# The first keys loaded in fp32 by SyncE's queue, a later running sum, and a reordered opening, in a fused forgetting-attention and MLP kernel

## The chip, the cores and the metric

The kernel runs on one core of one Trainium2 chip. The metric is the device time of one execution in microseconds (us). The time before is 321.48 us, the median of 3 runs (321.39 to 321.61). A profile is one further execution, recorded by the hardware; its span runs from the first to the last instruction.

## The reference

The first half is attention with a forget gate: B=8 batches, H=8 heads, S=576 positions, D=64. The second half is an MLP with a tanh-approximated GELU over the 4608 tokens, 512 to 2048 to 512. All inputs and outputs are fp32.

```python
scores = scale * np.matmul(q, k.transpose(0, 1, 3, 2))
log_f = np.log(np.clip(f, 0.0001, 1.0))
cum = np.cumsum(log_f, axis=-1)
decay = cum[:, :, :, None] - cum[:, :, None, :]
scores = np.where(causal, -1000000000.0, scores + decay)
attn = np.exp(scores - max) ; attn = attn / (np.sum(attn, axis=-1) + 1e-09)
x = (attn @ v) with the heads side by side          # 4608 x 512
h = x @ w_in
out = gelu_tanh(h) @ w_out
```

## The kernel before

**Attention.** Four heads are one quad; a batch has two quads, and 16 quads in all are numbered i. For a quad, q and k are loaded by GpSimd's queue (`load_one`, L205), which casts fp32 to bf16 on the way, into one of two buffers each (`k_c`, `q_c`). VectorE transposes them in blocks of 32 (`transpose_words`, L211) into `kT` and `qT`. TensorE multiplies 32 of the 64 columns of D at a time for four heads side by side in the rows of its array (`scores`, L265), into two PSUM tiles; ScalarE takes the exponential (L291) into `pt`, bf16. The causal mask on the diagonal blocks is set on GpSimd (`mask`, L293) or by a product on VectorE (`mask_by_product`, L317). The decay needs no work per score: the factor exp(-cum) of each key is multiplied into the values (`make_vw`, L227) and into the weights of the denominators (`w_bf`), and the factor of the query cancels in the division. For it, f is loaded by SyncE, clamped on VectorE, put through a logarithm on ScalarE (`logs`, L721), summed along each row on VectorE (`running_sums`, L725), transposed on TensorE (`cum_tiles`, L743) and exponentiated on ScalarE (`make_w`, L749). The denominators (`denominators`, L362) and the outputs (`attn_out`, L380) are products with `pt` in which the four heads lie side by side in the columns of the array; VectorE divides and writes x, transposed, into `xT`.

**MLP.** Tokens are worked on in nine chunks of 512. The first product runs by `mlp_in` (L388) or, for the first chunk, in halves of 256 tokens by `mlp_in_half` (L422); ScalarE takes the GELU into `gT`. The second product runs in units, for chunk 0 by `mlp_out` (L679) and from then on by `seven_products` (L603), which makes seven block products in place of eight and needs sums of the blocks of `gT` and `w_out` on VectorE. From chunk 2 on part of the first product uses the same scheme (`two_units`, L526).

**Order.** Each engine works through its own queue in order, and a program order written out by hand sets all of them. `setup` (L701) issues the first loads and constants; then `run` (L842) goes through tables of words: `FRONT` (L71) for everything up to chunk 2, `SECOND` for chunk 2, and so on. A word is an operation with its arguments. Those that matter here:

- `S.i.r` scores of round r of quad i; `H.i.r.g` the same for two of the four heads. Their matmuls use 32 rows of the array and 128 columns.
- `D`, `V`, `v` denominators and outputs (an argument 0 or 1 at the end is the first 256 or the last 320 positions); 128 rows and 32 columns, or one.
- `M` mask on GpSimd, `m` on VectorE. `VW` weighted values on GpSimd, `vw` on VectorE.
- `j`, `J`, `I` first product of the MLP; `GJ` its GELU where it is put off, `RJ` a copy of its raw sum. `F.c.n` n units of the second product of chunk c with 128 columns at a time, `f.c.n` the same units with four matmuls of 32 columns each.
- `B.n.c` n matmuls of c columns on zeros into a spare tile (`keep_busy`, L253); `BK` the same behind a transposed k (L259). They have no result.
- `SC` running sum, `CT` and `CE` its transposition and exponentials, `W`/`w` the cast of the factors. `TK`, `TQ` transpositions of k and q.
- Loads: `LK`, `LQ` of k and q; `LP` and `LC` of one piece of 128 positions of v for batch 0 and 1, by GpSimd's queue; `LV` of half of a v, by SyncE's; `WI`, `WO` pieces of w_in and w_out, by GpSimd's.
- `CL`, `cl` copy of one block of the weighted values, on VectorE or ScalarE; `UW`, `PW` a sum of blocks of w_in, on VectorE or GpSimd; `U` sums of w_out; `UT` and `tr` make the triangles for the mask.

The opening of `setup` and the issue of a load of k or q:

```python
nc.sync.dma_start(out=f_sb, in_=f.rearrange("b h s -> (b h) s"))          # L702
load_one(k, k_c, 0)                                                       # L704
load_one(q, q_c, 0)
```

PSUM has two tiles for scores (and the first product), one for products of a whole quad (the idle matmuls write it too) and two for the rest.

## Time and profile before

| | us |
|---|---|
| median of 3 runs | 321.48 |
| the profiled execution | 320.93 |
| its span | 319.2 |
| TensorE matmul busy | 313.2 (98%) |
| VectorE busy | 243.0 (76%) |
| ScalarE busy | 212.6 (67%) |
| GpSimd busy | 109.3 (34%) |

Matmuls are pipelined and their ends are modelled, so a busy TensorE is not one at its peak; starts are measured. The page cuts the span into 40 slices and shows in tenths how busy each engine was. The chain that ended last is followed back from the last instruction, each step to what released it. A row of a timeline gives start, duration, engine, line, operation, output<-input, the count of instructions merged into it, and in brackets how long the engine was idle before it and what ended that. PE is TensorE, PEld its weight loads, DVE VectorE, ACT ScalarE, POOL GpSimd, SP SyncE. A transfer has the time from its issue to its landing.

### The profile page before, as it was taken

What the parts mean: (1) busy time and instruction counts of PE and PEld (TensorE: products, weight loads), DVE (VectorE), ACT (ScalarE), POOL (GpSimd) and SP (SyncE); (2) the same over time, 40 slices, a digit from 0 to 9 for tenths busy, and PEclk for the clock granted to TensorE, in tenths of its full rate; (3) what the DMA queues carried; (4) which work ended last, traced back from release to release, by engine and by line L of the source; (5) the groups of instructions that cost most, each with busy time, mean ns of one, the idle gap of its engine ahead of it and who ended that gap; (6) DMA issues with size and microseconds to landing.
All of it is one profiled execution on the core that took longest, in us unless ns stands there. A gap on an engine that the chain in (4) does not pass through costs nothing.

```text
span 319.2 us, 11780 instructions
## 1 busy us (share of the span) xinstructions
PE 313.2 (98%) x5318; PEld 219.1 (69%) x5318; DVE 243.0 (76%) x369; ACT 212.6 (67%) x246; POOL 109.3 (34%) x148
## 2 busy tenths in 40 slices
PE   7999999999999999999999999999999999999996
PEld 2467734545676577776788878767776786688785
DVE  7777438598878889879877987599876866597674
ACT  3766885966766876877767866787596744836610
POOL 8799541920340416410851075305610140000000
PEclk9999999999999999999999999999999999999999
DMA  7999999985253901593139411961001111010203
GB/s 126 222 203 204 208 227 218 176 156 103 45 105 103 215 7 39 120 206 74 39 87 224 89 39 36 213 152 38 5 34 67 35 36 35 28 40 2 101 33 100
DMA packets 47490, 33.41 MB, mean 105 GB/s; under 512 B 29776, under 2 KB 42192, under 8 KB 47440
## 3 DMA queue, kind: packets, MB, share of 16 engines
q0 software_dynamic: 9632, 15.99, 28.8%
q1 hardware_dynamic: 37664, 16.60, 19.5%
q8 instruction: 41, 0.67, 0.9%
q10 hardware_dynamic: 144, 0.07, 0.1%
q14 instruction: 9, 0.07, 0.1%
HBM read 36.85 MB, written 9.44 MB: 145 GB/s over the span
## 4 chain that ended last, share of the span: by engine, by line
PE 94%; DMA 3%; POOL 1%; DVE 1%; issue 0%; DVEq 0%; POOLq 0%
PE ps_w L617 31%; PE ps_h L401 20%; PE ps_q L537 10%; PE po L353 9%; PE ps_s L283 9%; PE pso L690 5%; PE ps_h L437 5%; PE ps_u L485 4%; DMA v_nat<-in_v_dram 3%; PE po_m L339 1%; PE ps_p L617 1%; POOL v_nat L184 0%; PE ps_o L353 0%; DVE usum L417 0%; POOL q_c L207 0%
## 5 line engine op out<-in xcount | busy, mean ns | idle before, releaser
L291 ACT ACTIVATE pt<-ps_s 128x1024 bf16<-128x1024 f32 (+2 forms) x100 | 94.1, 991 | 38.2 <-PE ps_s L283 36.6
L297 POOL TENSOR_SCALAR_AFFINE_SELECT pt<-pt 128x512 bf16<-128x512 bf16 (+3 forms) x73 | 45.9, 638 | 95.4 <-ACT pt L291 72.4
L401 PE MATMUL ps_h<-xT,w_in_sb 128*128 128x512 bf16 (+1 forms) x320 | 66.9, 358 | 0.0
L401 PEld LDWEIGHTS <-w_in_sb 128*128 128x128 bf16 x320 | 31.2, 98 | 26.1 <-issue 0.2
L617 PEld LDWEIGHTS <-gT 128*32 128x32 bf16 (+1 forms) x1171 | 44.0, 97 | 5.9 <-issue 2.4
L409 ACT ACTIVATE gT<-ps_h 128x1024 bf16<-128x1024 f32 x34 | 34.6, 1017 | 20.3 <-PE ps_h L401 20.1
L617 PE MATMUL ps_w<-w_out_sb,gT 128*32 128x256 bf16 (+1 forms) x996 | 42.5, 273 | 0.0
L617 PEld LDWEIGHTS <-gsum 128*32 128x32 bf16 (+1 forms) x903 | 35.3, 97 | 3.7 <-issue 1.3
L283 PE MATMUL ps_s<-qT,kT 32*128 32x64 bf16 (+5 forms) x896 | 35.4, 261 | 0.6 <-DVE qT L214 0.4
L553 DVE TENSOR_TENSOR usnap<-ps_q,usnap 128x1024 f32<-128x1024 f32 x15 | 17.9, 1220 | 17.3 <-PE ps_q L537 12.7
L617 PE MATMUL ps_w<-usum,gsum 128*32 128x256 bf16 (+1 forms) x749 | 30.1, 273 | 0.0
L283 PEld LDWEIGHTS <-kT 32*128 32x128 bf16 x896 | 16.3, 92 | 17.0 <-issue 10.2
L231 POOL TENSOR_TENSOR vw<-v_nat,wT 128x1280 bf16<-128x1280 f32 (+1 forms) x12 | 27.3, 2274 | 0.9 <-DMA v_nat<-in_v_dram 0.6
L634 DVE COPY snap<-ps_w 128x512 f32<-128x512 f32 x32 | 21.8, 680 | 6.7 <-PE ps_w L617 6.5
L214 DVE STREAM_TRANSPOSE kT<-k_c 128x576 f32<-128x576 f32 x16 | 19.4, 1243 | 6.8 <-DMA k_c<-in_k_dram 6.8
L385 DVE TENSOR_TENSOR xT<-po,rb 128x576 bf16<-128x576 f32 x26 | 19.5, 751 | 5.1 <-PE po L353 4.9
L548 ACT ACTIVATE gT<-usnap 128x1024 bf16<-128x1024 f32 x15 | 15.8, 1053 | 11.0 <-DVE usnap L553 10.7
L214 DVE STREAM_TRANSPOSE qT<-q_c 128x576 f32<-128x576 f32 x16 | 19.7, 1243 | 4.4 <-DMA q_c<-in_q_dram 4.4
L353 PE MATMUL po<-pt,vw 128*32 128x64 bf16 (+4 forms) x624 | 22.4, 278 | 0.0
L207 POOL DMA_DIRECT2D k_c<-in_k_dram x16 | 9.0, 565 | 35.7 <-DVE kT L214 23.5
L353 PEld LDWEIGHTS <-vw 128*32 128x32 bf16 x672 | 14.6, 97 | 9.3 <-issue 2.6
L537 PEld LDWEIGHTS <-w_in_sb 128*128 128x128 bf16 x160 | 15.6, 98 | 2.1
(134 smaller groups left out, 482.9 us busy)
## 6 DMA issues: line engine op xcount, KB each, us to landing
out_dram<-o_st SPq DMA_DIRECT2D x35, 256.0 KB, 2.2
k_c<-in_k_dram POOLq DMA_DIRECT2D x16, 288.0 KB, 5.7
q_c<-in_q_dram POOLq DMA_DIRECT2D x16, 288.0 KB, 5.7
v_nat<-in_v_dram SPq DMA_DIRECT2D x16, 256.0 KB, 4.9
v_nat<-in_v_dram SPq DMA_DIRECT2D x20, 128.0 KB, 5.4
v_nat<-in_v_dram POOLq DMA_DIRECT2D x8, 256.0 KB, 8.8
w_in_sb<-in_moe_w_in_dram POOLq DMA_DIRECT2D x8, 256.0 KB, 7.4
w_out_sb<-in_moe_w_out_dram POOLq DMA_DIRECT2D x4, 512.0 KB, 10.5
```

The source lines that it names most:

```text
L214: return nc.vector.transpose(out=dst.rearrange("p s c -> p (s c)").bitcast(FP32) .rearrange("p (t a) -> p a t", a=n), in_=src.rearrange("p ...
L231: return eng.tensor_mul(vw[i % 2][:, t0:t1], vb[:, t0:t1, h0:h0 + 4, :], wT[:, i, t0:t1, :].unsqueeze(3).to_broadcast([128, t1 - t0, 4, D]))
L283: nc.tensor.matmul(tiles[h // 2][:, h % 2, c0:c0 + nq], key_columns(i, key, h, c), qq[32 * h:32 * h + 32, q0:q0 + nq, c], start=(c == 0 an ...
L291: nc.scalar.activation(p[:, 2 * g:2 * g + 2, off:off + n], t[:, :, 0:n], AF.Exp, scale=scale)
L297: nc.gpsimd.affine_select(out=x, in_=x, compare_op=ALU.is_ge, fill=0.0, base=0, pattern=pattern, channel_multiplier=-1)
L353: nc.tensor.matmul(po[r0:r0 + w.shape[-1], 448 + q0:448 + q0 + nq], w, p[:, h, col:col + nq], start=(key in (0, "low")), stop=(key in ("lo ...
L385: nc.vector.tensor_mul(xT[:, 2 * u + x, r0 + s0:r0 + s1], po, rbs[i, part])
L401: nc.tensor.matmul(ph[:, j, n * cols:(n + 1) * cols], w_in_sb[:, dt, 128 * ft:128 * ft + 128], xT[:, dt, h0:h0 + cols], start=(dt == 0 and ...
L409: nc.scalar.activation(gelus(c, 2 * pr, 2), ph, AF.Gelu_apprx_tanh)
L537: nc.tensor.matmul(ps[:, k, HC * n:HC * n + HC], w[:, d, 128 * n:128 * n + 128], x[:, d, :], start=(first and n == 0 and d == 0), stop=(d ...
L617: nc.tensor.matmul(ps[c0:c0 + width, n, cols[0]:cols[1]], x[:, j, 128 * n + c0:128 * n + c0 + width], w[:, j, cols[0]:cols[1]], start=(fir ...
L634: copy(kept[name], ps)
```

## The change

The first k (quad 0) is no longer loaded by GpSimd's queue. SyncE's queue loads it in fp32, ahead of f, into a stretch of `gT` that nothing else uses yet, and ScalarE copies it from there into `k_c[0]` in bf16, ahead of the logarithm of f. The clamp of f stays where it was in VectorE's order, behind the constants of `setup` and ahead of the first transposition. In `FRONT`, `SC` moves from ahead of the first k's transposition to behind the first q's; the loads of v and the weights, the idle matmuls, the score words and the units of the second product up to chunk 2 stand in another order. Some words change engine: `UW.2.1` becomes `PW.2.1`, `M.2.0` becomes `m.2.0`, `CL.2` and `CL.5` become `cl.2` and `cl.5`. Of the 64 units of chunk 0's second product, 48 in place of 45 are `f`. There are more idle matmuls: 12 in place of 7 of 128 columns, 3 in place of none of 256, 21 in place of 20 of 512, and 7 in place of 5 behind a transposed k. Everything else in `FRONT` is the same set of words.

```diff
--- before.py
+++ after.py
@@ -69,18 +69,19 @@
     ON_ACT = ()
 
     FRONT = """
-        LP.1 LP.4 SC LP.0 WI.0 B.8.512 B.1.512 CT TK.0 CE.1 TQ.0 CE.0 B.2.512 LP.3 B.1.128 BK.0.2 B.1.512 WI.5 B.1.512 S.0.0 TK.1 M.0.0 B.1.128
-        B.1.128 WI.1 WI.2 B.1.128 BK.0.1 B.3.512 H.0.2.1 B.1.128 BK.0.1 H.0.2.0 WI.3 H.0.1.0 W.0 LP.2 TQ.1 D.0.0 H.1.0.0 vw.0.0 B.1.128 B.2.512
-        BK.1.1 H.1.0.1 M.1.0 H.0.1.1 B.1.512 M.0.1 vw.1.0 V.0.1.0 B.1.128 B.1.512 V.0.0.0 H.0.3.0 UT D.1.0 j.0.0.4 V.1.0.0 V.1.1.0 H.1.3.1 WI.4 WI.7
-        H.0.3.1 WI.6 j.0.0.4 j.0.0.8 H.1.1.0 RJ.0.0 M.0.3 WO.0 H.1.1.1 vw.0.1 LC.1.1 D.0.1 j.0.1.8 H.1.3.0 M.1.1 WO.1 M.1.3 H.1.2.1 V.0.0.1 VW.1.1
-        V.0.1.1 UW.2.1 W.1 LQ.2 H.1.2.0 J.0.2 LK.2 LK.3 WO.2 D.1.1 j.0.1.8 GJ.0.1 V.1.0.1 V.1.1.1 TK.2 J.0.3 tr WO.3 J.1.1 TQ.2 GJ.0.0 LQ.3 U.0
-        J.1.3 J.1.2 J.1.0 F.0.1 f.0.3 LC.1.2 LC.1.0 f.0.2 S.2.0 TK.3 X f.0.2 PW.2.2 F.0.7 LC.1.3 F.0.1 S.2.2 f.0.2 F.0.1 TQ.3 f.0.2 LC.1.4 LQ.4 LK.5
-        f.0.4 S.2.1 F.0.1 f.0.4 LV.2.1 F.0.1 LK.4 F.0.3 M.2.2 F.0.1 vw.2 m.2.1 F.0.2 CL.2 LV.2.0 S.3.0 f.0.1 M.2.0 f.0.2 D.2 f.0.3 S.3.1 TQ.4 f.0.1
-        LQ.6 VW.3 f.0.4 M.3.0 f.0.1 V.2.0 TK.4 S.3.2 f.0.6 V.2.1 m.3.1 S.4.1 f.0.4 LQ.5 f.0.1 H.4.2.0 f.0.2 M.3.2 H.4.2.1 cl.3 D.3 VW.4 H.4.0.0
-        M.4.2.3 H.4.0.1 V.3.1 LK.6 v.3.0 f.0.1 F.0.1 I.1.2 I.1.0 TQ.5 U.1 TK.5 TQ.6 vw.5 I.1.5 UW.2.4 I.1.1 LV.3.1 LV.3.0 I.1.3 TK.6 U.3 I.1.4 U.2
-        m.4.2.2 I.1.6 I.1.7 LK.7 X F.1.1 CL.5 F.1.2 M.4.1 G.0 G.1.1.2 F.1.4 cl.4 F.1.9 S.5.0 F.1.12 UW.2.3 m.4.0 F.1.4 M.5.0 F.1.4 F.1.5 S.5.1 D.4
-        F.1.5 LQ.8 F.1.2 F.1.4 S.5.2 V.4.0 f.1.1 M.5.1 M.5.2.2 M.5.2.3 LK.8 f.1.11 V.4.1 S.6.0 f.1.3 D.5 LQ.7@m.3.1 M.6.0 f.1.10 S.6.1 vw.6 f.1.1
-        V.5.1 f.1.1 F.1.9 CL.6 M.6.1 F.1.2 S.6.2 m.6.2.3 f.1.1 V.5.0 f.1.4 F.1.2 m.6.2.2
+        B.1.128 LP.0 B.1.512 LP.3 B.1.256 TK.0 LP.1 B.8.512 B.1.512 B.1.128 TQ.0 B.2.512 B.1.256 B.1.128 B.1.128 SC TK.1 BK.0.2 BK.0.1
+        B.1.512 S.0.0 B.1.512 WI.1 WI.0 BK.0.1 B.1.128 TQ.1 B.1.128 CT H.0.2.1 WI.2 BK.0.1 LP.2 CE.0 H.0.2.0 B.3.512 B.1.128 B.1.128 W.0
+        BK.0.1 CE.1 B.1.128 H.1.0.1 H.0.1.0 B.1.128 M.0.0 B.1.256 B.2.512 LP.4 vw.0.0 D.0.0 H.1.0.0 WI.3 V.0.0.0 H.0.1.1 WI.4 V.0.1.0 M.1.0
+        H.0.3.0 BK.1.1 B.1.128 B.1.512 B.1.128 M.0.1 vw.1.0 H.1.2.0 D.1.0 WI.5 H.0.3.1 V.1.1.0 WI.6 LQ.2 V.1.0.0 LK.2 B.1.512 H.1.3.0 WI.7
+        M.0.3 j.0.0.4 j.0.0.4 H.1.1.0 H.1.3.1 UT j.0.0.8 RJ.0.0 D.0.1 tr WO.0 LC.1.4 H.1.1.1 H.1.2.1 j.0.1.8 M.1.3 M.1.1 GJ.0.0 j.0.1.8
+        J.0.2 vw.0.1 V.0.1.1 VW.1.1 V.0.0.1 D.1.1 V.1.0.1 V.1.1.1 LQ.3 J.0.3 GJ.0.1 J.1.0 WO.1 TQ.2 J.1.2 LK.3 F.0.1 J.1.1 F.0.1 W.1 WO.2
+        PW.2.1 WO.3 LC.1.0 J.1.3 LQ.4 f.0.5 U.0 LC.1.3 LC.1.2 LC.1.1 TK.2 S.2.0 TK.3 F.0.1 LK.4 X F.0.4 f.0.4 TQ.3 f.0.2 m.2.0 LK.5 S.2.2
+        M.2.2 X f.0.9 PW.2.2 S.2.1 f.0.1 F.0.8 LV.2.1 m.2.1 S.3.0 f.0.1 vw.2 D.2 f.0.3 M.3.0 cl.2 LV.2.0 f.0.3 S.3.1 V.2.0 f.0.4 LV.3.0 TQ.4
+        f.0.1 LQ.5 f.0.1 TK.4 S.3.2 TK.5 V.2.1 f.0.2 VW.3 M.3.2 f.0.3 cl.3 UW.2.4 LK.6 f.0.1 S.4.1 f.0.4 m.3.1 VW.4 f.0.2 H.4.2.0 D.3
+        H.4.0.0 H.4.0.1 V.3.1 f.0.1 v.3.0 vw.5 LQ.6 TQ.5 f.0.1 H.4.2.1 F.0.1 I.1.0 I.1.4 U.1 I.1.5 LV.3.1 U.2 F.1.1 U.3 I.1.6 I.1.1 G.0 TK.6
+        cl.4 I.1.2 I.1.3 I.1.7 TQ.6 G.1.1.2 F.1.9 cl.5 F.1.3 M.4.2.3 LK.8 F.1.2 S.5.0 F.1.5 LK.7 F.1.3 m.4.2.2 F.1.5 UW.2.3 m.4.0 M.4.1
+        F.1.5 M.5.0 F.1.2 S.5.1 D.4 LQ.7@m.3.1 F.1.17 M.5.1 S.5.2 LQ.8 M.5.2.2 M.5.2.3 f.1.3 V.4.0 f.1.10 V.4.1 S.6.0 M.6.0 f.1.2 D.5 f.1.11
+        S.6.1 f.1.1 V.5.1 M.6.1 F.1.2 vw.6 CL.6 F.1.4 F.1.5 S.6.2 m.6.2.3 f.1.5 V.5.0 m.6.2.2 F.1.2
     """
 
     SECOND = """
@@ -207,6 +208,14 @@
         return nc.gpsimd.dma_start(
             out=dst[i % 2].rearrange("p a d -> p (a d)"),
             in_=src[b, h0:h0 + 4].rearrange("h (p a) d -> (h p) (a d)", p=32))
+
+    first = gT.rearrange("p f n -> p (f n)").bitcast(FP32)[:, 0:S * D // 32]
+
+    def load_first():
+        nc.sync.dma_start(out=first, in_=k[0, 0:4].rearrange("h (p a) d -> (h p) (a d)", p=32))
+
+    def cast_first():
+        nc.scalar.copy(k_c[0].rearrange("p a d -> p (a d)"), first)
 
     def transpose_words(src, dst):
 
@@ -699,9 +708,9 @@
 
 
     def setup():
+        load_first()
         nc.sync.dma_start(out=f_sb, in_=f.rearrange("b h s -> (b h) s"))
         nc.scalar.preload_act_table_set("natural_log_exp_and_others")
-        load_one(k, k_c, 0)
         load_one(q, q_c, 0)
         make_identity(nc, ident_f32)
         load_one(k, k_c, 1)
@@ -715,6 +724,7 @@
             nc.vector.memset(t_[:, 0:64], 0.0)
             nc.vector.memset(t_[:, 64 + S:], 0.0)
         zeros()
+        cast_first()
         logs()
         idle_ps.append(psO.tile([128, 1024], FP32, name="idle_ps", tag="po"))
```

## The prediction

> **What bounds the kernel now.** I read the page first for the chain that ended last, then that chain in order of time, then the timeline of each engine over the first 60 us, then the transfers in single moments of the opening.
>
> ```profile
> PE 94%; DMA 3%; POOL 1%; DVE 1%; issue 0%; DVEq 0%; POOLq 0%
> ```
>
> TensorE carries 94% of the chain. The 3% of DMA are one piece of it (start, duration, what):
>
> ```profile
> 5.66 8.76 DMA v_nat<-in_v_dram
> 14.52 0.70 DVE vw L231
> ```
>
> This is the third piece of v and VectorE's weighting of it; behind it comes the first product with values. The timeline of VectorE, then of TensorE (start, duration, engine, line, operation, output<-input, count):
>
> ```profile
> 3.50 0.45 DVE L722 TENSOR_SCALAR f_all<-f_all 64x576 f32<-64x576 f32 x1
> 4.70 1.35 DVE L726 TENSOR_TENSOR_SCAN f_all<-ones_f,f_all 64x576 f32<-64x576 f32 x1 [0.75 <-ACT f_all L723]
> 5.97 1.23 DVE L214 STREAM_TRANSPOSE kT<-k_c 128x576 f32<-128x576 f32 x1
> 7.39 1.26 DVE L214 STREAM_TRANSPOSE qT<-q_c 128x576 f32<-128x576 f32 x1 [0.19 <-DMA q_c<-in_q_dram]
> ```
>
> ```profile
> 12.11 0.35 PE L339 MATMUL po_m<-pt,w_bf 128*32 128x256 bf16 x8
> 12.57 0.52 PE L283 MATMUL ps_s<-qT,kT 32*128 32x256 bf16 x8
> 13.02 0.66 PE L256 MATMUL idle_ps<-idle 128*128 128x128 bf16 x3
> 13.52 0.38 PE L262 MATMUL idle_ps<-kT,idle 128*128 128x512 bf16 x1
> 13.83 0.97 PE L283 MATMUL ps_s<-qT,kT 32*128 32x256 bf16 x16
> 14.73 0.39 PE L256 MATMUL idle_ps<-idle 128*128 128x512 bf16 x1
> 15.27 0.35 PE L339 MATMUL po_m<-pt,vw 128*32 128x256 bf16 x8
> 15.55 0.45 PE L256 MATMUL idle_ps<-idle 128*128 128x128 bf16 x2
> 15.92 0.35 PE L339 MATMUL po_m<-pt,vw 128*32 128x256 bf16 x8
> ...
> 29.51 8.91 PE L437 MATMUL ps_h<-xT,w_in_sb 128*128 128x256 bf16 x80
> ```
>
> A start minus the start before it is what a step costs on TensorE. Until 15.27 us it waits or runs idle matmuls (L256, L262). From 15.27 us on each start follows the end of the step before, but for two idle matmuls of 0.37 us (15.55 to 15.92). So the time is set by how late the dense part begins and by what is added to it or cut from it. All real work behind it is the same in both kernels, so the gain is limited to a part of these first 15 us.
>
> **The change, part by part.** *The loads.* First GpSimd's issues in the timeline, then three rows of transfers, each taken in the moment of its issue (last number: us from issue to landing); the GB/s row has 40 slices over the first 4 us.
>
> ```profile
> 1.30 0.71 POOL L207 DMA_DIRECT2D k_c<-in_k_dram  x1 [0.79 <-POOLq L878]
> 2.01 0.54 POOL L207 DMA_DIRECT2D q_c<-in_q_dram  x1
> ...
> 17.95 2.14 POOL L196 DMA_DIRECT2D w_in_sb<-in_moe_w_in_dram  x3
> ```
>
> ```profile
> GB/s 0 0 0 0 0 0 0 0 0 0 0 0 0 0 0 0 0 0 0 0 0 69 138 207 92 276 346 277 254 23 0 46 69 92 161 138 161 115 207 115
> ...
> k_c<-in_k_dram POOLq DMA_DIRECT2D x1, 288.0 KB, 4.6
> ...
> q_c<-in_q_dram POOLq DMA_DIRECT2D x1, 288.0 KB, 5.4
> ...
> w_in_sb<-in_moe_w_in_dram POOLq DMA_DIRECT2D x1, 256.0 KB, 8.6
> ```
>
> GpSimd's first k lands at 1.30+4.6=5.9 and the first q at 2.01+5.4=7.41: 1.5 us apart for 288 KB written in bf16, 576 KB read, or some 390 GB/s read. SyncE's queue moves f from 2.1 to 3.0 us, at 250 to 350 GB/s at its best; f is used at 3.50, half a microsecond after its last byte.
>
> The first k in fp32 has 576 KB. At 280 GB/s alone it takes 2.1 us from 2.1 us on, so it lands at 4.7. If from 2.7 us on it shares the engines evenly with GpSimd's first q, it lands near 6. I take 5.0, near the lower end, since GpSimd's queue shows at most 207 GB/s in the fourth microsecond. f stands behind it in the same queue: 5.2 to 6.7; I take 5.7, which is 2.2 us later than now.
>
> The cast on ScalarE is new. A row for it:
>
> ```profile
> 20.97 1.94 ACT L291 ACTIVATE pt<-ps_s 128x1024 bf16<-128x1024 f32 x2 [0.74 <-PE ps_s L283]
> ```
>
> 0.97 for 1024 columns makes about 1.1 for 1152: 5.05 to 6.15. VectorE's clamp of f (0.45) stands ahead of the first k's transposition in its queue and gates it: 5.75 to 6.2. Both paths meet at 6.2. Then k (1.23) to 7.45 and q (1.26) to 8.7; the first q, now in the first slot of GpSimd's queue, lands between 5.9 and 7.4, in time. Now the first q ends at 7.39+1.26=8.65. What the moved running sum no longer holds up (1.35 ahead of k), the later f and the cast use up: nil, from -0.4 (k at 4.3, f at 5.2) to +0.6 (f at 6.3).
>
> *VectorE behind it.* Running sum to 10.05, second k to 11.3, second q to 12.55. Now the scores that need the second q start at 12.57. VectorE's waits for k and q in between are what takes up the sum. Nil again.
>
> *TensorE up to the first product with values.* Behind the second q it now has two score words on different heads, so different rows of the array (two on the same heads took 0.90, 13.83 to 14.73; one takes 0.45, 12.57 to 13.02; I take 0.85), four fillers with 1408 columns (0.21 per 512, with a change of shape 0.7), the denominators (0.46, 12.11 to 12.57) and one score word (0.45). 12.6 and 2.5 make 15.1. ScalarE also has the exponentials of the running sums, and then the mask casts, inside the score phase; score words wait for its two buffers. By 15.1 the first is over; behind it ScalarE mostly waits for TensorE, so I cost the casts nothing. Without that cover, score words slip by their length.
>
> *The third v.* The wanted pieces are now first and third, and the one between is whole, not the 64-row half: about 0.5 more. The queue starts earlier by one load, and the first k fills its ramp. By the GB/s row, 2.1 to 3.0 us moved 187 of 390 GB/s and 3.0 to 4.0 moved 110 written, so 220 of 390 read: 0.9 us unused. I take 0.65 of it as gained, bounds 0 and 0.9. Landing 14.42+0.5-0.65=14.3, weighting 0.7, product at 15.05. Two separate chains thus give 15.1; bounds 14.6 and 15.7.
>
> *From there to the 80-matmul block (29.51 now).* Before: 14.24 us from 15.27. After: the same words, plus a score word that stood ahead of the product (0.45), fillers of 0.77 in place of 0.27, less one change of shape (0.12): 15.07. 15.1+15.07=30.2, that is 0.65 late.
>
> *The last piece of w_in.* The block's third matmul needs it. It is the third of a run of three (0.71 each) from 17.95: issued at 19.38, landed 8.6 later, 27.98. Now the third q and the third k go ahead of it: 3.0, less the 0.65: 30.3. Wanted at 30.4. Bounds 30.1 and 31.0; I take a stall of 0.1.
>
> *Changes of shape behind the block.* What one costs on TensorE:
>
> ```profile
> 52.63 1.48 PE L690 MATMUL pso<-w_out_sb,gT 128*32 128x512 bf16 x24
> 53.94 0.85 PE L353 MATMUL po<-pt,vw 128*32 128x512 bf16 x24
> ...
> 58.00 1.26 PE L690 MATMUL pso<-w_out_sb,gT 128*32 128x512 bf16 x20
> 59.20 0.63 PE L283 MATMUL ps_s<-qT,kT 32*128 32x320 bf16 x8
> ```
>
> With the same shape behind them, 24 matmuls take 1.31, so 0.218 for four; with another behind them, 20 take 1.20, so 0.11 for the change. I take 0.12. Going through the words (S and H are 32x128; D, V, v and f are 128x32; F, J, j, I and B are 128x128), neighbours differ 42 times from the block to chunk 2 before and 38 times after: -0.5. Three output units move from F to f at the same price.
>
> *Small words.* They move between engines beside a dense TensorE:
>
> ```profile
> 25.04 2.06 DVE L467 TENSOR_TENSOR wsum<-w_in_sb 128x512 bf16<-128x512 bf16 x1
> ...
> 34.39 1.18 POOL L469 TENSOR_TENSOR wsum<-wsum,w_in_sb 128x512 bf16<-128x512 bf16 x1
> ```
>
> One sum of w_in leaves VectorE (2.06) for GpSimd (1.18, ahead of the last w_out load); one mask goes from GpSimd to VectorE; two small copies from VectorE to ScalarE. TensorE's dense stretch covers them. If that goes, the first product of quad 2 waits for its weighted v, which I place 0.5 ahead of its use.
>
> **The sum.** 0.65 at the block, 0.1 stall, -0.5 shapes: about +0.3. The profiled execution took 320.93 for its span of 319.2, 0.55 under the median of 321.48. So 321.2 beside it, 321.8 as a median. A measurement of this kernel tells about 0.2% (0.64 us) from no change.
>
> **A rule that speaks against the gain.** In the rows, GpSimd's loads land at one rate from 5.9 us on, and the GB/s row has room ahead of that. The Trainium skill (DMA: Bandwidth & Descriptors, "Issuing engines are not separate DMA queues") says that loads started by different engines run on the same 16 DMA engines, and that starting them on several saves only the time of issue. The landings agree; the ramp of the first two microseconds is what the trace sets against it. The second rival is what the rule would do here.
>
> **Rivals.** *The opening gains (faster).* k lands at 4.3, f at 5.2, the third v at 14.0: first product at 14.6, block at 29.7, shapes -0.5: -0.3; with the fillers behind the product shadowing waits that TensorE now has, down to -0.8. So 320.7 to 321.2. For it: the room in the ramp. Against it: VectorE's and TensorE's own chain reaches 15.1 without any transfer of v. It decides if the first q's transposition ends by 8.3.
>
> *The transfers gain nothing.* Third v at 14.96, product at 15.7, block at 30.8, w_in at 31.0 in time: 1.3-0.5=+0.8, so 322.3. For it: one landing rate from 5.9 us on. Against it: the ramp.
>
> *A late f (slower).* f stands behind k in its queue and its clamp ahead of the transposition in VectorE's. The five VectorE steps from there follow without a gap, so past 5.75 each microsecond of f is one of the end: f at 7.0 gives +1.3 on the base, 323.1. The last w_in, landed at 31.7, would do the same. For it: four times f's bytes stand ahead of it. Against it: that queue's 280 GB/s. It decides from f at 6.3.
>
> **How the numbers follow.** Base (own range 321.2 to 322.3) 0.40; opening gains 0.22; no gain 0.18; late f 0.20. The range 320.6 to 323.3 leaves out the end of the last case and little below. Faster by over 0.2% (under 320.84): half of the gaining case and some for what I don't see, 0.15. Slower by over 0.2% (over 322.12): the late f, most of the third case and a tenth from the base's top, 0.43. Within: 0.42.
>
> **What would show it.** First q's transposition ending at 8.7, the second's at 12.55, first product with values at 15.1, the 80-matmul block at 30.2 and not released by w_in, dense from there. It is wrong if the clamp starts after 6.3, if TensorE has gaps behind 16 us, or if the output units or quad 2's product wait for w_out or v.

## The result and the profile after

The changed kernel is slower by 0.5%: 322.54 us against 321.05 for the kernel before, timed beside it, a ratio of 1.0051 with a 95% interval of 1.0038 to 1.0063. Its profiled execution took 321.55 us for a span of 319.8, against 320.93 and 319.2. It is the fastest of its 22 executions; the next one took 322.07. So the profile shows the change at its best, and a part of the loss has to be looked for in other executions.

The page's chain that ended last, by engine and then by line, shows what is new on the path:

```profile
PE 91%; DVE 4%; ACT 1%; DMA 1%; issue 1%; SPq 0%; DVEq 0%
PE ps_w L626 30%; PE ps_h L410 19%; PE ps_q L546 10%; PE po L362 9%; PE ps_s L292 9%; PE pso L699 4%; PE ps_u L494 4%; PE ps_h L446 3%; DMA f_all<-in_f_dram 1%; DVE vw L240 1%; PE po_m L348 1%; PE idle_ps L265 1%; DVE xT L394 1%; ACT pt L300 1%; PE ps_p L626 1%
```

The piece of v is gone from it. In its place stand the load of f and a weighting of v on VectorE. The timelines of the profiled execution show both, first ScalarE, then VectorE, then TensorE, then GpSimd (start, duration, engine, line, operation, output<-input, count, idle time before and its releaser; lines are about nine further down than before):

```profile
4.69 1.15 ACT L218 CAST k_c<-gT 128x1152 bf16<-128x1152 f32 x1 [2.61 <-DMA gT<-in_k_dram]
```

```profile
5.51 0.45 DVE L732 TENSOR_SCALAR f_all<-f_all 64x576 f32<-64x576 f32 x1 [2.00 <-DMA f_all<-in_f_dram]
5.88 1.25 DVE L223 STREAM_TRANSPOSE kT<-k_c 128x576 f32<-128x576 f32 x1
6.98 1.24 DVE L223 STREAM_TRANSPOSE qT<-q_c 128x576 f32<-128x576 f32 x1
...
10.34 1.23 DVE L223 STREAM_TRANSPOSE qT<-q_c 128x576 f32<-128x576 f32 x1
...
23.84 3.75 DVE L240 TENSOR_TENSOR vw<-v_nat,wT 128x768 bf16<-128x768 f32 x1
```

```profile
8.27 0.52 PE L292 MATMUL ps_s<-qT,kT 32*128 32x256 bf16 x16
...
14.15 0.35 PE L348 MATMUL po_m<-pt,vw 128*32 128x256 bf16 x8
...
27.65 0.95 PE L348 MATMUL po_m<-pt,vw 128*32 128x320 bf16 x32 [0.76 <-DVE vw L240]
...
30.64 5.41 PE L446 MATMUL ps_h<-xT,w_in_sb 128*128 128x256 bf16 x48
36.11 3.87 PE L446 MATMUL ps_h<-xT,w_in_sb 128*128 128x256 bf16 x32
```

```profile
23.70 1.62 POOL L306 TENSOR_SCALAR_AFFINE_SELECT pt<-pt 128x512 bf16<-128x512 bf16 x3
25.28 1.49 POOL L240 TENSOR_TENSOR vw<-v_nat,wT 128x768 bf16<-128x768 f32 x1
```

The opening is faster than before: f has landed by 5.5, the first scores start at 8.27 (8.71 before), and the first product with values at 14.15 (15.27). Then it is lost again. VectorE's weighting of the last piece of the first v starts at 23.84 and takes 3.75 us; the same instruction took 0.96 before, where GpSimd's masks stood at other moments. VectorE's timeline before:

```profile
21.93 0.96 DVE L231 TENSOR_TENSOR vw<-v_nat,wT 128x768 bf16<-128x768 f32 x1 [0.30 <-DMA v_nat<-in_v_dram]
```

Now GpSimd has just begun three masks (23.70) and goes straight on with a weighting of its own (25.28), until 26.77. VectorE ends at 27.59, 0.82 after that, and TensorE, which has had nothing to do for 0.76 us (1.06 from one start to the next), goes on at 27.65. The 80-matmul block starts at 30.64 in place of 29.51.

By stages, with the starts of TensorE's steps in the two profiled executions:

| | before | after | stage before | stage after |
|---|---|---|---|---|
| first product with values | 15.27 | 14.15 | 15.27 | 14.15 |
| 80-matmul block | 29.51 | 30.64 | 14.24 | 16.49 |
| first product of chunk 1 | 64.76 | 64.98 | 35.25 | 34.34 |
| chunk 2 | 99.46 | 100.13 | 34.70 | 35.15 |

So -1.12, +2.25, -0.91 and +0.45 make +0.67, and the span is 0.6 longer. What the change gains at the opening and on balance behind the block (0.46), it loses between the two, and more.

### The profile page after: what moved, and what is told of

Same layout as the page of the kernel before. It is cut to its first block, busy times and chain, and to the rows that moved or that the text cites. A ratio compares the mean times of both kernels' runs of the same rounds, so it can differ in the third digit from the quotient of the medians.

```text
span 319.8 us, 11801 instructions
## 1 busy us (share of the span) xinstructions
PE 312.0 (98%) x5320; PEld 220.6 (69%) x5338; DVE 243.8 (76%) x367; ACT 214.4 (67%) x249; POOL 109.4 (34%) x146
## 4 chain that ended last, share of the span: by engine, by line
PE 91%; DVE 4%; ACT 1%; DMA 1%; issue 1%; SPq 0%; DVEq 0%
PE ps_w L626 30%; PE ps_h L410 19%; PE ps_q L546 10%; PE po L362 9%; PE ps_s L292 9%; PE pso L699 4%; PE ps_u L494 4%; PE ps_h L446 3%; DMA f_all<-in_f_dram 1%; DVE vw L240 1%; PE po_m L348 1%; PE idle_ps L265 1%; DVE xT L394 1%; ACT pt L300 1%; PE ps_p L626 1%
## 5 line engine op out<-in xcount | busy, mean ns | idle before, releaser
L306 POOL TENSOR_SCALAR_AFFINE_SELECT pt<-pt 128x512 bf16<-128x512 bf16 (+3 forms) x71 | 45.1, 646 | 96.1 <-ACT pt L300 67.6
L410 PE MATMUL ps_h<-xT,w_in_sb 128*128 128x512 bf16 (+1 forms) x308 | 65.6, 357 | 0.9 <-issue 0.2
```

What stands on the lines that cost most here:

```text
L306: nc.gpsimd.affine_select(out=x, in_=x, compare_op=ALU.is_ge, fill=0.0, base=0, pattern=pattern, channel_multiplier=-1)
L410: nc.tensor.matmul(ph[:, j, n * cols:(n + 1) * cols], w_in_sb[:, dt, 128 * ft:128 * ft + 128], xT[:, dt, h0:h0 + cols], start=(dt == 0 and ...
```

## The experiments

Each kernel was profiled once and timed against the kernel before on the same chip. The table has the landing of what gates the first transposition (f, or k where it lands behind f), three starts on TensorE, the granted clock's half-speed stretch if there was one behind the first full one, and the ratio with its interval. Times in us, from the traces; a landing is the issue plus the time to landing, to 0.1.

| kernel | f or k landed | first scores | block | chunk 2 | half clock | ratio |
|---|---|---|---|---|---|---|
| before | k 5.9 | 8.71 | 29.51 | 99.46 | none | 1 |
| after, the profile above | f 5.5 | 8.27 | 30.64 | 100.13 | none | 1.0051 (1.0038 to 1.0063) |
| a_again | f 7.0 | 10.46 | 33.39 | 102.88 | 8.57 to 11.98 | 1.0068 (1.0050 to 1.0086) |
| a_vw_early | f 6.6 | 9.46 | 30.89 | 100.39 | none | 1.0059 (1.0030 to 1.0089) |
| a_words_only | k 5.4 | 8.26 | 30.34 | 99.84 | none | 1.0021 (1.0008 to 1.0035) |
| a_load_sc | f 7.6 | 10.46 | | | 10.06 to 30.54 | 1.0074 (1.0050 to 1.0099) |
| a_f_first | k 6.6 | 10.23 | 35.32 | 104.81 | 9.93 to 16.76 | 1.0156 (1.0119 to 1.0192) |
| a_fill | f 7.4 | 10.22 | 32.58 | 102.27 | none | 1.0075 (1.0056 to 1.0094) |
| a_ff_vw_cl5 | k 7.0 | 11.31 | 33.34 | 102.42 | 9.48 to 12.89 | 1.0103 (1.0065 to 1.0141) |
| w_vw_cl5 | k 5.9 | 8.70 | 30.62 | 100.04 | none | 1.0015 (1.0004 to 1.0027) |
| a_q_late | f 6.0 | 9.70 | 32.03 | 101.53 | none | 1.0047 (1.0028 to 1.0066) |
| a_fact_vw_cl5 | f 6.2 | 8.96 | 30.55 | 100.63 | none | 1.0012 (0.9994 to 1.0030) |
| a_fact_oldwords | f 6.4 | 13.96 | 35.05 | 105.13 | 9.09 to 15.92 | 1.0164 (1.0141 to 1.0188) |
| b_middle | k 5.5 | 9.83 | 30.10 | 99.69 | see there | 0.9995 (0.9978 to 1.0012) |

**The changed kernel again** (a_again), unaltered.

> The changed kernel once more, unaltered, as the measure for the other three and as a second profile. The first profile shows one long gap of TensorE behind the opening: the weighting of v for positions 256 to 575 on VectorE (vw.0.1) took 3.75 us, where the same shape took 0.96 in the kernel before, and TensorE stood still for 1.1 us of it. Blocking theory: VectorE could not run while three masks and the other weighting of v ran back to back on GpSimd (23.70 to 26.77), so the long weighting and the gap come again, and the time is again 0.3 to 0.6% over the kernel before. Chance theory: the long weighting belongs to that one execution; it lasts about 1 us here and the gap is somewhere else.

Measured: 1.0068, six executions from 322.77 to 324.68, the profiled one 324.30. VectorE's and TensorE's timelines:

```profile
6.99 0.45 DVE L732 TENSOR_SCALAR f_all<-f_all 64x576 f32<-64x576 f32 x1 [3.48 <-DMA f_all<-in_f_dram]
```

```profile
8.66 1.44 PE L271 MATMUL idle_ps<-kT,idle 128*128 128x512 bf16 x3 [2.29 <-DVE kT L223]
...
10.46 0.83 PE L292 MATMUL ps_s<-qT,kT 32*128 32x256 bf16 x16
```

This is the execution that the profile above doesn't show. k lands nearly as early as there (its cast starts at 4.88 against 4.69), so the cast is done by 6.0; f lands 1.5 later, VectorE waits 3.48 for it, and the first scores start 2.19 later. The transfers in the same two microseconds of both profiles show where it is held up (queue, packets, MB, share of 16 engines; q1 is SyncE's queue, q0 GpSimd's). The changed kernel's first profile from 5 to 7 us, then this one's:

```profile
q0 software_dynamic: 187, 0.39, 108.8%
```

```profile
q0 software_dynamic: 124, 0.26, 92.0%
q1 hardware_dynamic: 5, 0.01, 3.0%
```

In the first, SyncE's queue has nothing left at 5 us. Here five packets are left, the last of f, and they take until 6.64: the packet records show rows starting at 5.81, 6.08 and 6.35, 0.27 apart, where a row took 0.09 while the queue had the engines for itself. The Trainium skill (DMA: Bandwidth & Descriptors, "Queues, rings and completion order") says that each DMA engine takes turns between the queues that have work for it, a packet at a time. The spacing agrees: behind GpSimd's bulk, a few leftover rows of f wait for a turn each. Whether any are left when GpSimd's bulk starts differs from execution to execution: f landed at 5.5, 6.6, 7.0, 7.4 and 7.6 in the five profiles with this load order.

f isn't the only load that is late in such an execution. GpSimd's first q is issued at 1.30 in all five. Its transfer, in the changed kernel's first profile and then in this one (last number: us from issue to landing):

```profile
q_c<-in_q_dram POOLq DMA_DIRECT2D x1, 288.0 KB, 5.0
```

```profile
q_c<-in_q_dram POOLq DMA_DIRECT2D x1, 288.0 KB, 6.9
```

So q lands at 6.3 there and at 8.2 here, and at 8.1 to 8.5 in the other three profiles with a late f. In a_q_late, below, q lands at 8.4, f at 6.0 doesn't gate, and the first scores start at 9.70. By that, some 1.2 of the 2.19 lost here would be lost with f on time too (an estimate from these two profiles). GpSimd's queue itself moved 0.26 MB in the two microseconds, in place of 0.39, and five packets of f can't account for that. Taking turns explains the spacing of f's last rows; why all transfers are slower in these executions isn't shown.

The half clock is the second loss. TensorE idles 2.29 us, and the windows of the profile (window, length, then busy time of the engines, granted clock, DMA share, GB/s) show it granted half speed from 8.57 to 11.98:

```profile
8.00:9.00 1.00, 0.34 (x1) 0.10 (x1) 1.00 (x2) 0.15 (x1) 0.51 (x1) 0.78 1.03 184
9.00:10.00 1.00, 1.00 (x4) 0.30 (x2) 1.00 (x2) 0.00 (x0) 0.27 (x2) 0.50 1.09 265
```

It is no part of the usual execution. The mean granted clock is on record for each: under 0.999 in only three of the changed kernel's 22, its longest (324.69 to 326.77), and in two of the six here. (This mean doesn't show half speed ahead of the first full one: b_middle, below, has 1.000 and ran at half speed until 9.95.)

**The weighting of v earlier** (a_vw_early), parts of two lines:

```diff
-  H.1.3.1 UT j.0.0.8 RJ.0.0
+  H.1.3.1 UT vw.0.1 j.0.0.8 RJ.0.0
-  J.0.2 vw.0.1 V.0.1.1
+  J.0.2 V.0.1.1
```

> The changed kernel with vw.0.1 moved up, from behind J.0.2 to ahead of the fourth part of j.0.0, where VectorE idles for 2.1 us (19.3 to 21.5) and GpSimd issues loads. The v it needs had landed at 19.6. Blocking theory: the weighting lasts about 1 us, the gap of 1.1 us at 26.4 goes, and with it part of the slips in the products behind (0.4): 1.1 to 1.5 us less than the changed kernel, at or under the kernel before. Load theory (the late f and the cast are what costs): no difference over 0.3 us.

VectorE's timeline, then TensorE's:

```profile
20.43 0.99 DVE L240 TENSOR_TENSOR vw<-v_nat,wT 128x768 bf16<-128x768 f32 x1
```

```profile
27.63 1.22 PE L348 MATMUL po_m<-pt,vw 128*32 128x320 bf16 x40
...
30.89 1.38 PE L446 MATMUL ps_h<-xT,w_in_sb 128*128 128x256 bf16 x11
```

The weighting takes 0.99 again and the gap is gone: 40 matmuls in 1.30 (27.63 to 28.93) in place of 2.25. From the first scores to the block it is 21.43 in place of 22.37. So the trace shows the blocking and its price of 0.95. The times alone don't separate it: six of the twelve executions lie between 321.50 and 322.14, below all six of a_again, but six between 323.72 and 327.38. The profile is one of the short ones, with f at 6.6; no long one was profiled. The mean granted clock splits the twelve in the same way: 0.999 or 1.000 in the six short ones, 0.984 to 0.995 in the six long ones. So the half clock goes with the long executions; that a late load brought it is not shown for them.

**The new words with the old loads** (a_words_only): the first k again in bf16 by GpSimd's queue, no cast, f alone on SyncE's.

```diff
-        load_first()
+        load_one(k, k_c, 0)
-        cast_first()
```

> The new words with the old load: the first k again by GpSimd's queue in bf16 with the cast in the transfer, no cast on ScalarE, f alone on SyncE's queue. Load theory: f is 2 us earlier, so this is faster than the changed kernel by 0.5 us or more. Opening theory: the first k lands at 5.9 in place of 5.85 after its cast, but every later load of GpSimd's queue is about a load later (1 to 1.5 us); first scores 0.3 to 0.5 us later, first product with values 0.8 to 1.3 later, and since the blocked weighting of v hangs on GpSimd's masks, which follow the scores, the end 0.3 to 1.0 us later than the changed kernel.

Measured 1.0021, less than half of what the whole change costs (1.0051, and 1.0068 in a_again, which ran beside this one). So the larger part of the loss is the load path. The weighting on VectorE wasn't blocked in this execution; GpSimd's timeline, then VectorE's:

```profile
24.03 2.35 POOL L306 TENSOR_SCALAR_AFFINE_SELECT pt<-pt 128x512 bf16<-128x512 bf16 x3
```

```profile
24.48 1.04 DVE L240 TENSOR_TENSOR vw<-v_nat,wT 128x768 bf16<-128x768 f32 x1
```

VectorE came 0.45 behind the first mask in place of 0.14, went in ahead of the next one, and GpSimd's masks took 2.35 instead of 1.62. Which engine was kept out was settled here by 0.3 us.

**The new loads with the old words** (a_load_sc), but with the running sum and what follows it behind the first q's transposition and the first score word:

```diff
-  LP.1 LP.4 SC LP.0 WI.0 B.8.512 B.1.512 CT TK.0 CE.1 TQ.0 CE.0 B.2.512
+  LP.1 LP.4 LP.0 WI.0 B.8.512 B.1.512 TK.0 TQ.0 SC B.2.512
-  S.0.0 TK.1
+  S.0.0 CT CE.0 CE.1 TK.1
```

> The old words with the new load and the running sum behind the first q's transposition (its transposition on TensorE and its exponentials behind the first scores); all else as in the kernel before. Opening theory: the load alone is a gain. First scores at about 8.3 in place of 8.7, third v landed 0.9 to 1.4 us earlier, first product with values at 14 to 14.8 in place of 15.27; the end 0.3 to 1.0 us under the kernel before. Load theory: at or over the kernel before, since f and the cast are late and the exponentials of the sums now stand among those of the scores.

Measured 1.0074, as much as the whole change. f landed at 7.6. This profiled execution (331.07 us) had half the clock for 20 us, behind an idle stretch of TensorE of 3.09 us, so nothing later is read from it. Seven of the eight executions have a mean granted clock of 0.969 to 0.995; the one with 1.000 took 321.36, as long as the kernel before (321.33). So with the old words, which have fewer idle matmuls, the loss goes with the half clock, and a cost of the load path without it isn't shown here.

**f ahead of k in SyncE's queue** (a_f_first):

```diff
-        load_first()
         nc.sync.dma_start(out=f_sb, in_=f.rearrange("b h s -> (b h) s"))
+        load_first()
```

> The changed kernel with two lines of its opening swapped: SyncE's queue loads f first and the first k in fp32 behind it. Late-f theory: f lands at 3.5 to 3.7 as in the kernel before, in every execution; k has f's 147 KB ahead of it and lands at 5.0 to 5.6, the cast on ScalarE ends at 6.1 to 6.8 and now sets the first transposition; the first scores start at 8.6 to 9.3, TensorE has no idle stretch of 2 us behind 6 us and its granted clock stays at 1.00. Ratio 1.000 to 1.004 (321.3 to 322.6), with a smaller spread than the unaltered change. Rival, the words alone cost it all: ratio 1.005 or more, as before. Rival, fp32 by two queues is slow whatever stands first: k lands behind 6.5 and the first scores at 10 or later.

The expectation failed: 1.0156. f lands at 3.5, but k, now second, at 6.6 in place of the 5.0 to 5.6 that I gave it. ScalarE's and TensorE's timelines:

```profile
6.66 1.15 ACT L218 CAST k_c<-gT 128x1152 bf16<-128x1152 f32 x1 [4.56 <-DMA gT<-in_k_dram]
```

```profile
9.15 0.81 PE L271 MATMUL idle_ps<-kT,idle 128*128 128x512 bf16 x3 [2.11 <-DVE kT L223]
10.23 0.83 PE L292 MATMUL ps_s<-qT,kT 32*128 32x256 bf16 x16
```

Whatever stood second in SyncE's queue met GpSimd's bulk. For k it is worse than for f, since the cast of 1.15 stands behind it. That isn't the whole loss: from the first scores to the block it took 25.09 against 22.37, with half the clock from 9.93 to 16.76, and all six executions have a mean granted clock of 0.984 to 0.995. GpSimd's bf16 load of k, which the change gave up, landed at 5.4 to 5.9 without a cast.

**More idle matmuls in the opening** (a_fill):

```diff
-  SC TK.1 BK.0.2 BK.0.1
+  SC TK.1 B.8.512 BK.0.2 BK.0.1
```

> The changed kernel with eight more idle matmuls of 512 columns (some 1.7 us) ahead of the first idle matmul that waits for the transposed k. They fill the stretch from 6.4 us on in which TensorE has nothing while f is late. If the half clock that the profiles of two late executions show (from 8.57 to 11.98 us in one, for 20 us in the other) follows from that idle stretch, it doesn't appear here although f lands at 6.5 to 7.7; the ratio falls from 1.007 to some 1.004. If the half clock has another cause, it appears again and the ratio stays at 1.006 to 1.008. If f is early (5.5), the fillers end at 8.1, before the first scores, and cost nothing.

VectorE's timeline, TensorE's, and a window:

```profile
7.46 0.45 DVE L732 TENSOR_SCALAR f_all<-f_all 64x576 f32<-64x576 f32 x1 [3.96 <-DMA f_all<-in_f_dram]
```

```profile
9.14 0.81 PE L271 MATMUL idle_ps<-kT,idle 128*128 128x512 bf16 x3 [0.67 <-DVE kT L223]
10.22 0.52 PE L292 MATMUL ps_s<-qT,kT 32*128 32x256 bf16 x16
```

```profile
9.00:10.00 1.00, 0.86 (x4) 0.29 (x3) 1.00 (x2) 0.00 (x0) 0.30 (x1) 1.00 1.08 274
```

f is later than in a_again, TensorE's idle stretch is 0.67 in place of 2.29, and the clock stays full, in all six executions (0.999 or 1.000 in the mean). This agrees with the half clock following from the idle stretch. From the first scores to the block it takes 22.36, to 0.01 what the changed kernel's first profile has (22.37); a_again with its half clock took 22.93. So the half clock costs some 0.6 behind the first scores, by one profile of each, and the late loads cost their full delay. The ratio, though, didn't fall to 1.004: it is 1.0075, and f was as late as ever in the profile (7.4, with q at 8.3).

**f first, the weighting earlier, one copy back on VectorE** (a_ff_vw_cl5): the edits of a_f_first and a_vw_early, and `CL.5` in place of `cl.5`.

> The changed kernel with f ahead of k in SyncE's queue, the weighting of the last piece of the first v put back ahead of the last part of the first product for half the first chunk (so that it runs before GpSimd's three masks and weighting), and the copy of quad 5's block on VectorE again. Theory: the three costs that the traces show (late f 0.8 to 1.4 us, TensorE's gap of 1.06 us when VectorE is kept out, 0.41 us at the second score word of quad 5) are gone; what stays is the score word and the fillers ahead of the first product with values, less the changes of shape. Ratio 0.997 to 1.001. Rival, the gaps are taken up by other waits of the opening: 1.002 to 1.004, like the new words with the old loads (1.0021).

1.0103, for the reason that sank a_f_first: k landed at 7.0, the first scores started at 11.31. From there to the block it is 22.03.

**The new words, mended, with the old loads** (w_vw_cl5): the same two edits of words on a_words_only.

> The loads of the kernel before (f first on SyncE's queue, the first k in bf16 on GpSimd's, no cast) with the new order of the words, the weighting of the last piece of the first v moved ahead and the copy of quad 5's block on VectorE. The new words alone had 1.0021 (1.0008 to 1.0035). Theory: the copy on VectorE takes the wait of 0.41 us at the second score word of quad 5 away and the earlier weighting takes the chance of a blocked VectorE away: 0.999 to 1.001. Rival, the words cost what they cost by the later first product of the MLP (30.34 against 29.51 us): 1.002 as before.

1.0015, not told apart from 1.0021. The wait at quad 5's second score word does go, as TensorE's timelines show, first of the changed kernel, then of this one:

```profile
83.86 0.63 PE L292 MATMUL ps_s<-qT,kT 32*128 32x64 bf16 x14 [0.21 <-ACT pt L300]
...
93.58 0.63 PE L292 MATMUL ps_s<-qT,kT 32*128 32x64 bf16 x16
```

```profile
83.43 0.63 PE L292 MATMUL ps_s<-qT,kT 32*128 32x64 bf16 x16
...
93.15 0.98 PE L292 MATMUL ps_s<-qT,kT 32*128 32x64 bf16 x16
```

But 0.35 of the 0.41 comes back ten microseconds later, at the next quad's score word (0.98 for 0.63), so chunk 2 starts 35.07 behind the first product of chunk 1, against 35.15. Score words wait for ScalarE's exponentials there, and a copy less on ScalarE only moves the place.

**GpSimd's queue later** (a_q_late): the identity is made twice ahead of the first q.

```diff
-        load_one(q, q_c, 0)
         make_identity(nc, ident_f32)
+        make_identity(nc, ident_f32)
+        load_one(q, q_c, 0)
```

> The changed kernel in which GpSimd makes its 64x64 identity twice and only then issues the first q, so that its queue starts some 0.85 us later; SyncE's queue is unaltered. Theory of alternation: the rows of f that SyncE's queue still has to move when GpSimd's queue starts go one by one between GpSimd's packets (0.27 us apart in place of 0.09), and the last of them makes f late. With GpSimd's packets from 4.8 us on, f is through: it lands at 5.3 to 5.6 in every execution, VectorE's clamp starts by 5.6, the first transposition by 6.0; the first q lands at 7.0 to 7.4 and becomes the limit of its own transposition; first scores 8.3 to 8.8, ratio 1.003 to 1.005 and a small spread. Rival, f is late for what it has ahead of it in its own queue alone: it lands at 5.5 to 7.7 as before, and the ratio stays at 1.005 to 1.007 or above, since all later loads start later too.

VectorE's timeline:

```profile
6.03 0.64 DVE L733 TENSOR_SCALAR f_all<-f_all 64x576 f32<-64x576 f32 x1 [2.52 <-DMA f_all<-in_f_dram]
6.60 1.23 DVE L223 STREAM_TRANSPOSE kT<-k_c 128x576 f32<-128x576 f32 x1
8.38 1.26 DVE L223 STREAM_TRANSPOSE qT<-q_c 128x576 f32<-128x576 f32 x1 [0.55 <-DMA q_c<-in_q_dram]
```

From 5 us on no packet of SyncE's queue is left, as the theory of taking turns has it, and f lands at 6.0, earlier than in four of the five profiles with an earlier q. The size was off: I expected 5.3 to 5.6, but k itself landed 0.5 later (5.3). And here q is what the first scores wait for, until 9.70: it landed at 8.4, where I had 7.0 to 7.4. The later issue need not be the reason, since q landed at 8.1 to 8.5 in those four profiles too, issued 0.62 earlier. The ratio of 1.0047 is inside the expectation.

**f by ScalarE's queue** (a_fact_vw_cl5), with the words of w_vw_cl5:

```diff
+        nc.scalar.dma_start(out=f_sb, in_=f.rearrange("b h s -> (b h) s"))
         load_first()
-        nc.sync.dma_start(out=f_sb, in_=f.rearrange("b h s -> (b h) s"))
```

> The changed kernel with f loaded by ScalarE's queue, ahead of its table load, at the same time as k by SyncE's; the weighting of the last piece of the first v moved ahead and the copy of quad 5's block on VectorE, as in the kernel with f first (1.0103). Theory of alternation: f's 64 rows and k's 128 now alternate from 2.1 us on, before GpSimd's packets come, so f lands at 3.5 to 4.5 and k at 4.7 to 5.3 in every execution; the first transposition starts at 5.9 to 6.5, the first scores at 8.3 to 8.9, no half clock; ratio 0.998 to 1.002 against 1.0015 with the same words and the old loads. Rival, a third queue slows the other two: k lands behind 5.8 and the ratio is 1.004 or more.

VectorE's and TensorE's timelines:

```profile
6.20 0.45 DVE L732 TENSOR_SCALAR f_all<-f_all 64x576 f32<-64x576 f32 x1 [2.70 <-DMA f_all<-in_f_dram]
6.58 1.25 DVE L223 STREAM_TRANSPOSE kT<-k_c 128x576 f32<-128x576 f32 x1
```

```profile
7.88 0.81 PE L271 MATMUL idle_ps<-kT,idle 128*128 128x512 bf16 x3 [1.60 <-DVE kT L223]
8.96 0.52 PE L292 MATMUL ps_s<-qT,kT 32*128 32x256 bf16 x16
```

It is the best of the kernels that load k in fp32, 1.0012, with an interval that takes in 1; but it beats neither the kernel before nor, by more than the intervals, the same words with the old loads. My theory of the rows was half wrong: f did not move from 2.1 us on beside k. Its first packets are seen from 3.5 us on, 39 of them in the fourth microsecond and 40 in the fifth, and it is used at 6.20.

**The same loads with the old words** (a_fact_oldwords). The kernel that ran differs from its expectation in one point: the transposition of the running sum (`CT`) and its exponentials (`CE`) stood ahead of the first score word, right behind the moved `SC`.

> The new loads with f on ScalarE's queue, and the order of words of the kernel before except that the running sum stands behind the first q's transposition and its transposition and exponentials behind the first score word. By the theory of alternation f and k are early in every execution (f by 4.5, k by 5.3): the opening is 0.3 to 0.5 us ahead of the kernel before, and the rest is its order: ratio 0.998 to 1.000. Rival, the opening's gain is taken up by the third v, which the first product with values waits for (15.27 us before): 1.000. With f behind k in SyncE's queue the same words took 1.0074 (1.0050 to 1.0099).

```profile
10.48 0.77 PE L756 MATMUL cum_ps<-ident_f,f_all 64*128 64x64 f32 x5 [5.20 <-DVE f_all L735]
...
13.96 0.82 PE L291 MATMUL ps_s<-qT,kT 32*128 32x256 bf16 x16
```

The first row of TensorE's timeline is the result: TensorE works in order, so `CT` held it for 5.20 us, the first scores start 5.25 later than in the kernel before, half clock followed from 9.09 to 15.92, and the ratio is 1.0164. It says nothing on the expectation, but it prices the place of `CT`: the change's own order, with `CT` behind the first scores, has to go with its later `SC`. Whether the new loads can gain with the old words and f by ScalarE's queue was not tried.

**The change's middle alone** (b_middle): the kernel before up to the block and from the first product of chunk 1 on, the changed order between. One mask of a diagonal block of quad 4 (`M.4.2.3`) comes ahead of the scores of two of its heads here, so for these the causal mask of that block is left out; its instruction is still there.

> The kernel before, with its loads and its words up to the 80-matmul block of the first product, then the changed kernel's order from that block to the first product of chunk 1, then the words of the kernel before again. In the traces the stretch from the block to the first product of chunk 1 took 35.25 us before and 34.34 after; the opening ahead of it was 1.13 us longer after (and up to 4 us with a late f), and the stretch behind it 0.45 longer. Theory, the three stretches are independent of each other: the block starts at 29.5, the first product of chunk 1 at 63.9 and chunk 2 at 98.6, against 29.51, 64.76 and 99.46; ratio 0.997 to 0.998 (320.4 to 320.9), faster than both kernels. Rival, ScalarE or the loads of w_out, which the later opening of the changed kernel left time for, take the gain up: the first product of chunk 1 at 64.5 or later, ratio 0.999 to 1.001.

TensorE's timeline:

```profile
6.36 0.76 PE L748 MATMUL cum_ps<-ident_f,f_all 64*128 64x64 f32 x5 [1.07 <-DVE f_all L727]
...
7.98 1.06 PE L263 MATMUL idle_ps<-kT,idle 128*128 128x512 bf16 x2
8.84 1.06 PE L257 MATMUL idle_ps<-idle 128*128 128x512 bf16 x2
...
35.83 0.39 PE L691 MATMUL pso<-w_out_sb,gT 128*128 128x512 bf16 x1 [0.31 <-ACT gT L431]
```

The middle took 34.96 (30.10 to 65.06) and not 34.34: 0.31 are a wait for a GELU, which this order of the joint puts late. So the stretches are not independent, and 0.29 of the 0.91 is left. The opening, with no word altered, was 0.59 later at the block than in the profile of before: its matmuls of 512 columns run 0.43 apart, half speed, until full speed is first granted at 9.95; in the profile of before that was at 5.01, and they ran 0.21 apart. The ratio of 0.9995 tells nothing from 1.

## Why the prediction was right or wrong

**The outcome.** Forecast 321.8, range 320.6 to 323.3, slower the likeliest of three signs by a little: 322.54 is in the range and slower. As a change it is +1.5 on the 321.05 timed beside it, where the base case said +0.3 and the late f +1.6 (323.1 against 321.48). So it is not the base case, whose own range ended at 322.3, but for the most part the rival called a late f. Two of the signs that the prediction gave against itself came: the clamp started behind 6.3 in four of the five profiles of this load order, and TensorE had a gap behind 16 us. In the profiled execution, by the prediction's own sign (8.22, ahead of 8.3), it was the rival called the opening gains, until the weighting of v was kept out.

**The first q's transposition at 8.7, the second's at 12.55.** In the profiled execution 8.22 and 11.57, both better: f landed at 5.5 and not 5.7, k at 4.7 and not 5.0, and the cast took 1.15 for the estimated 1.1. The failed step is the term "f stands behind it in the same queue: 5.2 to 6.7; I take 5.7". One profile in five has it ahead of 5.7; the others have 6.6 to 7.6, three of them outside the bounds. The first q, "between 5.9 and 7.4, in time", failed beside it: 8.1 to 8.5 in the same four. The prediction shared the engines by bytes at the rates of the kernel before. What the packets show is a leftover of f between GpSimd's packets, and GpSimd's own queue slower by a third from 5 to 7 us (a_again).

**"Past 5.75 each microsecond of f is one of the end".** The rows bear it out along f's own path. With the clamp at 5.51, 6.60 (a_vw_early) and 7.46 (a_fill) the first scores start at 8.27, 9.46 and 10.22: 1.19 for 1.09, 1.95 for 1.95. And from the first scores to the block the distance is the same in the first and the last (22.37 and 22.36). What the rival left out is the late q, which in a_vw_early would by itself have held the first q's transposition to 8.1, where f held it to 8.18. It also left out the clock: where TensorE idled for over 2 us, half speed for 3.4 us or more adds to it, some 0.6 in a_again.

**The third v at 14.3 and the first product with values at 15.1.** 13.1 and 14.15 in the profiled execution, so the ramp was worth 1.9 there, not 0.65, and outside the bounds of 0 to 0.9. That was the exception: in a_again, a_vw_early and a_fill the third v landed at 14.2 to 14.3, as predicted, against 14.4 before.

**From there to the block, 15.07.** It took 16.49. The step that failed is "Small words ... TensorE's dense stretch covers them". It counts the words that change engine; the weighting of v stays on VectorE, but the new order puts it behind the first of three GpSimd masks, and it is put at nothing and not covered. It was kept out for 2.8 us and cost 0.95. That leaves 0.47: with the weighting moved (a_vw_early) the stage still takes 15.54 (15.35 to 30.89). From start to start its score words take 0.77 more than before (3.68 against 2.91, forecast 0.45) and its idle matmuls 0.60 more (0.97 against 0.37, forecast 0.50), the rest together 0.07 less (forecast 0.12). So the score word in its new place was the term that was too small. That the whole distance from the first scores to the block (21.43) is near the prediction's own (15.07 and 6.4, so 21.5) is luck: the part ahead of the product was 0.5 shorter than forecast. The row that warned was quoted: the sum of w_in that took 2.06 on VectorE, while GpSimd had masks. I took it for the price of the operation; the same sum at 71.93 us of that trace took 0.41.

**The last piece of w_in, a stall of 0.1.** It landed at 29.3, ahead of the block; no wait.

**Changes of shape behind the block, -0.5.** Block to chunk 2: 69.95 before, 69.49 after, so -0.46. As a sum it is right, but partly by luck, since it has two parts that it didn't name: -0.91 up to the first product of chunk 1 and +0.45 behind it, where a score word waits for ScalarE. The traces do have 42 changes of shape before and 38 with the new words (a_words_only): 27 and 23 in the first part, 15 in the second in both. Four at 0.12 are half of the 0.91; what the other half is, no run shows. w_vw_cl5 shows that this wait can't be taken away by moving one copy.

**What stays open.** Why f's leftover, and the pace of GpSimd's queue beside it, differ between executions of one program isn't shown. For the single execution the traces explain its time; how often each landing comes is known from five profiles only.

## What to carry to other kernels

When two loads gate an opening, the one that stands second in a queue meets the bulk of the other queues: putting f first only made k the late one (1.0156), and a queue of its own for f did best (1.0012), though not better than the old loads. A load that shares the DMA engines with a bulk transfer is costed by its last row, not by its bytes, and the gates behind it (here q) are costed too. Before an instruction with two SBUF inputs is moved on VectorE, look at what GpSimd does in that microsecond; and when a table says that an opening gained, take several executions before the gain is believed, since the profiled one may be the best of them.

## What the runs showed of the hardware

- **VectorE kept out by a run of GpSimd instructions.** 3.75 us for 0.96, through three masks and a weighting that followed each other without a gap; it ended 0.82 behind the last. The same length, 3.75, stands in a_again. The Trainium skill (SBUF — State Buffer, "Who interferes with whom") says that a VectorE instruction with two SBUF inputs contends with a GpSimd instruction that reads SBUF, and that the order of issue decides who waits. The traces agree, and add that the one kept out may lose against several instructions in a row: VectorE 0.13 to 0.16 behind the first mask lost in five profiles, 0.45 behind it won in one.
- **The clock.** Half speed came back in all five profiles in which TensorE idled for 2.1 us or more in the opening (2.11, 2.29, 2.70, 3.09, 5.20), and in none with up to 1.85. The stretches of 3.41 (8.57 to 11.98, 9.48 to 12.89), 6.83 (9.09 to 15.92, 9.93 to 16.76) and 20.48 (10.06 to 30.54) are one, two and six of the same length. The Trainium skill (TensorE: Matmul & The Clock Gate, "What's actually happening") speaks of a free-running window of 3413 ns, whose idleness or business sets the clock; the lengths agree. An idle stretch shorter than a window was enough here. Full speed itself first came at 5.0 in the profile of before and at 9.95 in b_middle, whose opening has the same words: 0.59 at the block between two executions of the same opening.
- **Second in a queue.** The load that stood second on SyncE's queue landed between 5.5 and 7.6, whether 147 KB (f) or 576 KB (k), while the first of 576 KB landed at 4.6 to 4.9 in the five profiles of the unaltered load order.
